# A re-planned order of a fused sparse-attention and gated-FFN kernel: free order among FFN products, the first eight in two column parts, smaller mask patterns, the fourth unit turned by crossbar transposes

## The chip, the core and the metric

One core of one Trainium2 chip runs the whole kernel in one launch. The metric is the device time of that launch in microseconds (us). The engines are PE (matrix products; its weight loads are listed as PEld), ACT, DVE and POOL for everything elementwise, and SP, which here only issues DMAs. Matrix results land in PSUM, which this kernel uses as eight buffers ("ps" 0 to 7).

## The reference, cut to what matters

There are 4 batches, 8 heads, 768 positions, head width 64. Keys come in chunks of 32. For each query and chunk an upper bound of the score is taken from the chunk's minimum and maximum; the six chunks with the highest bounds stay, and everything else, and the future, is masked.

```python
k_min, k_max = min and max of k over each chunk of 32 rows
ub = sum over d of maximum(q * k_min, q * k_max)      # bound per query and chunk
top_chunks = the 6 largest causal ub
scores = q @ k.T / 8, masked to the chosen chunks and to the past
attn = softmax(scores);  x = attn @ v                 # -> (3072, 512)
out = (sigmoid(x @ w_gate) * (x @ w_val)) @ w_out     # 512 -> 1536 -> 512
```

## The kernel before

**Units.** The 3072 rows are cut into eight units of 384 rows (three blocks of 128). Unit 0 holds the first block of batches 0 and 1 and a block 0 of batch 2, whose attention needs one key block and no selection (function first, L604). Units 1 to 7 do the selection and the attention over all earlier key blocks (attend, L847). After a unit's attention comes its FFN: for units 0 to 3 by plain products (ffn, L937, project_out, L968), for units 4 to 7 two units at a time with a Strassen-like scheme of seven products instead of eight (ffn_pair, L1016, project_pair, L1162), for which sums of weights (Sg, Sv, So) and of activations (T, S) are made on DVE or POOL.

**A unit's attention.** Keys and queries arrive as float32, are turned (units 1 and 2 by PE, kT and qT, through copies kn and qn; later batches by DVE's transposes) and copied as float16 into hk (keys) and hq (queries). Both have two halves of 64 rows: one holds the data, the other the mask. On the key side that is a fixed pattern (a large negative number where a chunk doesn't match its row), written once per batch parity, head half and pair parity: the eight hkp operations at L498, each 64 rows by 2 x 768 columns, all copied from the tile epat. On the query side it is the selection (ub, ubn, mx, ap, apt, hqm in choose, L789). A score product (sc, L863) then adds score and mask in one matmul; ACT takes the exponential (L874), POOL zeroes the future (cm, L880), PE multiplies with the values (pv, L896), DVE divides (rz, x, L913 to L915).

**Turning x for the FFN.** The FFN needs x with its 512 features on partitions. Units below XBAR = 4 are turned by PE: three transposes per head pair (xps, L929) and a copy of ACT or DVE (xT, L933). Units from 4 on are turned by a DMA transpose (L920), issued on SP.

**The FFN of units 0 to 3.** For each of 12 blocks of 128 hidden features, a product g of four matmuls of 384 columns (L952), tanh on ACT, a product v, and hg = (tanh + 1) * v on DVE (L964). All these products write a common key "ffn", so each depends on the one before: g0, v0, g1, v1, and so on, then the 9 groups o of the projection. All products read the whole xT, that is all blocks of the unit.

**Loads.** SP issues the loads of q, k and v and the stores, in one queue. The weights come as nine DMAs of POOL's queue that also convert to float16 (wg0 to wg2, wv0 to wv2, wo0 to wo2; a third of the features each); they wait until the first loads have landed (the after operations, L510).

**What sets the order.** Everything is an operation of a plan (Plan.add), with its readers, writers and the engines it may run on. The plan isn't scheduled at run time: the string ORDER (L97) names all 1982 operations in the order in which they are issued, for all engines at once, with the engine where it isn't the first one allowed (name@ENGINE) and the buffers (name:slot). Each engine executes its operations in this order and waits at each for what it needs. BEATS (L95) gives 13 groups of filler transposes of PE (beat0 to beat12, 78 in all, L473), whose results nobody reads; they keep PE running while it would wait at the start.

```python
BEATS = (20, 9, 8, 3, 3, 10, 5, 1, 2, 2, 6, 6, 3)
...
op = plan.add(f"g_{u.name}_{fb}", pe(650), product(g, wg16), reads=xt + [("wg", fb // 4)], writes=[g, "ffn"],
              prio=next_())
```

Of the kernel before, what the change touches and what calls it, by code (L numbers as in the profile page):

```python
# [15 lines left out]
XBAR = 4  # L16
# [85 lines left out]
kfT_0:5 kn_u1_1@POOL:1 qf16_0@DVE:0 qf0_1 qn_u2_3:4 kx1_u1_3 qn_u1_3:5 after3 vf_2:0 kf16_0:6 kxf0 hk1_u1_3@ACT
beat2:7 scf_0:0,4,1 v16_0_0 kT_u1_2:6 qf_u1_0 vf_1:1 kn_u2_0:0 hk0_u1_0 kx0_u1_2 hq0_u1_1@POOL expf_0_0 beat3:7
kT_u2_0:2 qT_u1_2:7 qf_u2_0:1 kf1_1 cmf_0_0 kt_u1_2:1 expf_0_1:2 q2_u2 hk1_u1_0@POOL beat4:0 pvf_0_0:3 kT_u1_1:0
qm_u1_1@ACT:0 hq1_u1_1@DVE kf0_2:0 qT_u1_3:4 after1 kx0_u1_0 vf1_2:1 qf0_2:1 kxf1:1 vc_2@ACT after6 qf1_2 qm_u1_0@ACT
kcr_f kx1_u1_2 cmf_0_1 kf1_2 qf_u1_2 kx1_u2_0:1 qf_u1_3 v11 beat5:1 pvf_0_1:7 k3_u2 qfT_1:6 kx0_u1_1 after4
qm_u1_3@ACT after5 wg0 kfT_1:4 q1_u2 rzf_0_1:0 kt_u2_0@DVE:0 qf16_1:5 k2_u2 hk0_u2_0 wv0 kt_u1_1:2 kf16_1@DVE:2 k1_u2
vf1_1:0 wg1 qm_u1_2 v_0_2:4 beat6:1 scf_1:4,6,1 qn_u2_2@DVE:3 hkp111 expf_1_1:3 v_0_3:3 beat7:1 qT_u2_2:5 qfT_2:1 hq0
vc_1@ACT kx1_u1_1 cmf_1_1 kfT_2:6 expf_1_0 rzf_0_0:1 kcr_u1@POOL xf_0_0:0 qf16_2:3 kf16_2@DVE:2 cmf_1_0 beat8:0
xpsf_0_0:3,0 xTf_0_0@ACT hkf0@DVE wv1 beat9:0 scf_2:6,1,2 qf_u2_2 xf_0_1:0 pvf_1_0:3 hk0_u1_2@ACT ub_u1:4,0 kx0_u2_0  # L110
hq0_u2_2@POOL expf_2_0 wg2 kn_u2_3@DVE:2 expf_2_1:1 hq0_u1_2@DVE pvf_1_1:6 rzf_1_0:0 hq0_u1_3 xf_1_0:1 cmf_2_1
ubn1_u1:0 qn_u2_1:0 vf1_3:3 rzf_1_1:0 hq1_u1_3 cmf_2_0 xf_1_1:2 beat10:5 qT_u2_1:0 xpsf_0_1:3 hq1 pvf_2_1:1
hq1_u2_0@POOL ubn0_u1 xpsf_1_1:6 xTf_0_1@ACT pvf_2_0:2 xpsf_1_0:7 kT_u2_3:5 hq0_u2_0 wv2 rzf_2_0:0 rzf_2_1:1
hk1_u2_0@ACT kn_u2_2@DVE:2 xf_2_0:1 wo0 qf_u2_1 v_0_1:0 xf_2_1:2 xTf_1_0@ACT beat11:4 xpsf_2_0:2 xTf_1_1@ACT ubm0_u1
xpsf_2_1:7 hk0_u1_1@ACT kn_u2_1@DVE:1 kT_u2_2:1 qT_u2_3:6 hk1_u1_1@POOL xTf_2_0 beat12:4 kT_u2_1:0 xTf_2_1 kt_u2_2:0
mx0_u1:0 wo1 hkp101@ACT g_u0_0:7,0,0 ap0_u1 wo2 apt0_u1:0 kx0_u2_2 qf_u2_3 v_u0_0:2 hq0_u1_0 hqm0_u1_2@DVE
g_u0_1:6,1,1 hq0_u2_3@POOL kx1_u2_1 hq1_u2_2@POOL v_u0_1:4 hk1_u1_2@POOL tanh_u0_1 tanh_u0_0 g_u0_2:3,2,2 hqm0_u1_0
hg_u0_1 kt_u2_1:1 v_u0_2:7 kx1_u2_2 hk0_u2_1@POOL tanh_u0_2 hg_u0_0 sc_u1_2_0:1,0 g_u0_3:3,1,3 hg_u0_2 exp_u1_2_0
k00_1:1 hq0_u2_1@DVE sc_u1_1_1:7,1 hk1_u2_1@ACT ubm1_u1 sc_u1_3_1:2,3 kx0_u2_1 cm_u1_2 sc_u1_2_1:1 sc_u1_0_2:4,2
exp_u1_3_1 v_u0_3:6 qm_u2_0@POOL:0 exp_u1_2_1 g_u0_4:2,2,4 tanh_u0_3 hq1_u1_0@POOL exp_u1_0_2 sc_u1_1_0:3 hk0_u2_2  # L120
tanh_u0_4 sc_u1_1_2:1 hkf1 sc_u1_3_0:4 exp_u1_3_0 v_u0_4:2 hk1_u2_2 kx1_u2_3 qm_u2_2@POOL exp_u1_1_0 g_u0_5:4,0,5
# [30 lines left out]
exp_u2_3_1 o1_u1_1 xf_3_1:0 k16_2_0@ACT:6 hqm0_u3_2 rz_u2_2:1 xpsf_3_1:7 kx1_2_1:1 xpsf_3_0:4 o2_u1_1 osb_u1_0 cm_u2_3
hq0_u3_2@POOL xTf_3_0@ACT xTf_3_1 sc_u3_1_0:2,1 ubn1_u3 v_2_2:4 osb_u1_1 sc_u3_0_2:4,2 x_u2_2:2 v16_1_3 exp_u3_0_2
out_u1_0 o0_u1_2:7,1 k16_2_2@DVE:4 exp_u2_2_2 v16_1_2 xps_u2_0:4 ubm1_u3 v_2_3:2 sc_u3_1_2:3 kt_2_3:0 pv_u2_3:6
xT_u2_0@ACT v16_1_0 pv_u2_2 exp_u3_1_0 q00_2 sc_u3_3_0:4,3 sc_u3_0_0:1 rz_u2_1:1 v16_1_1 x_u2_1:1 sc_u3_1_1:2
# [150 lines left out]
def kernel(  # L306
# [630 lines left out]
    def ffn(u, base, span):  # L937
# [4 lines left out]
        for fb in range(NFB):  # L942
# [6 lines left out]
            def product(t, w16, fb=fb):  # L949
                def emit(e):  # L950
                    for c in range(4):
                        nc.tensor.matmul(at(t), w16[:, c, 128 * fb:128 * fb + 128], at(u.xt)[:, c, :],  # L952
                                         start=(c == 0), stop=(c == 3))
                return emit
# [431 lines left out]
```

## Time and profile before

| what | us |
|---|---|
| times of three runs | 284.38, 285.82, 285.83 |
| median | 285.82 |
| the profiled execution | 284.64 |
| its span, first to last instruction | 282.9 |
| first FFN product (unit 0) starts | 31.05 |
| first projection of unit 0 starts | 50.8 |
| last product ends | 279.3 |

The profile is that of one execution. A stage is read from the busy times of the engines in a stretch of the span, and who waits for whom from the lists of waits. PE, DVE, ACT, POOL and SP run beside each other; an engine that is busy less than the others in a stage isn't what ends it. Matmuls overlap each other in PE's pipeline, so the distance of their starts, not their duration, is what one costs.

### The profile page before, as it was taken

The page shows a single profiled execution, that of the slowest core. Times are in us where ns is not written, and L with a number is a line of the kernel's source. Part 1 is how long each engine was busy: PE and PEld are TensorE (multiplying, and loading weights), DVE is VectorE, ACT ScalarE, POOL GpSimd, SP SyncE. Part 2 cuts the span into 40 slices and gives each one's busy share as a digit, 9 for nine tenths or more (in the row PEclk, how much of TensorE's full clock was granted, in tenths as well). Part 3 has the DMA queues.
Part 4 walks back from the last instruction along what each step waited for, and adds up shares of the span by engine and source line. Part 5 has one row for each costly group of instructions (what it writes and reads, how often), then busy time and mean ns, then how long its engine had stood idle before and what let it go on. Part 6 is the DMA issues. An engine that isn't in the chain of part 4 may idle for free.

```text
span 282.9 us, 7408 instructions
## 1 busy us (share of the span) xinstructions
PE 271.4 (96%) x2746; PEld 187.4 (66%) x2746; DVE 245.1 (87%) x665; ACT 215.5 (76%) x467; POOL 144.5 (51%) x221
## 2 busy tenths in 40 slices
PE   6998899999999999999999999999999999999994
PEld 5875565765666656754777666667666786676783
DVE  2788778529979999997998998999999999999983
ACT  4787897665667956877899998989999937778620
POOL 7468673245433765773567974415648310347020
PEclk9799999999999999999999999999999999999999
DMA  6999999999989999999920112200001013010005
GB/s 174 292 232 184 197 197 208 162 189 222 147 194 163 228 173 215 180 205 185 228 62 17 30 30 67 89 20 13 14 16 29 16 49 117 0 39 37 3 19 204
DMA packets 130035, 34.28 MB, mean 121 GB/s; under 512 B 118096, under 2 KB 127056, under 8 KB 130000
## 3 DMA queue, kind: packets, MB, share of 16 engines
q1 hardware_dynamic: 125248, 29.11, 48.9%
q0 software_dynamic: 4752, 4.72, 10.2%
q8 instruction: 21, 0.34, 0.5%
q14 instruction: 14, 0.11, 0.1%
HBM read 30.67 MB, written 6.29 MB: 131 GB/s over the span
## 4 chain that ended last, share of the span: by engine, by line
PE 77%; DVE 12%; ACT 5%; issue 3%; POOL 2%; POOLq 0%; DVEq 0%; ACTq 0%
PE g_u L952 11%; PE v_u L952 11%; PE sc_u L863 10%; PE o_u L983 8%; PE pv_u L896 6%; PE suo_u6u L1210 3%; PE suv_u6u L1069 3%; PE suo_u4u L1210 3%; PE sug_u6u L1069 2%; PE sug_u4u L1069 2%; PE suv_u4u L1069 2%; PE ube_u L801 2%; PE sro_u6u L1210 1%; PE sro_u4u L1210 1%; PE srv_u6u L1069 1%
## 5 line engine op out<-in xcount | busy, mean ns | idle before, releaser
L874 ACT ACTIVATE att_u<-sc_u 128x512 f16<-128x512 f32 (+3 forms) x184 | 90.6, 550 | 14.1 <-PE sc_u L863 13.0
L880 POOL TENSOR_SCALAR_AFFINE_SELECT att_u<-att_u 128x384 f16<-128x384 f16 (+1 forms) x56 | 29.0, 529 | 40.0 <-ACT att_u L874 34.8
L952 PE MATMUL g_u<-xT_u,wg 128*128 128x384 f16 x192 | 39.0, 326 | 1.0 <-DVE hg_u L964 0.6
L952 PE MATMUL v_u<-xT_u,wv 128*128 128x384 f16 x192 | 39.0, 326 | 0.0
L983 PE MATMUL o_u<-wo,hg_u 128*128 128x512 f16 x144 | 36.1, 379 | 0.0
L960 ACT ACTIVATE gate_u<-g_u 128x384 f16<-128x384 f32 x48 | 23.1, 494 | 12.3 <-PE g_u L952 10.6
L964 DVE SCALAR_TENSOR_TENSOR hg_u<-gate_u,v_u 128x384 f16<-128x384 f16 x48 | 25.2, 537 | 5.4 <-PE v_u L952 4.2
L896 PEld LDWEIGHTS <-att_u 128*128 128x128 f16 x640 | 25.3, 98 | 4.7 <-issue 0.2
L863 PE MATMUL sc_u<-hqo,hko 128*128 128x128 f16 (+2 forms) x220 | 27.9, 243 | 0.3 <-ACT att_u L874 0.2
L863 PE MATMUL sc_u<-hqe,hke 128*128 128x128 f16 (+2 forms) x220 | 27.4, 243 | 0.3 <-DVE ubn_u L812 0.3
L896 PE MATMUL pv_u<-v,att_u 128*128 128x65 f16 x640 | 27.6, 193 | 0.0
L952 PEld LDWEIGHTS <-wg 128*128 128x128 f16 x192 | 18.2, 98 | 11.9 <-issue 1.4
L952 PEld LDWEIGHTS <-wv 128*128 128x128 f16 x192 | 18.3, 98 | 11.1 <-DVE x_u L915 0.3
L863 PEld LDWEIGHTS <-hko 128*128 128x128 f16 x220 | 17.0, 98 | 7.3 <-issue 1.6
L863 PEld LDWEIGHTS <-hke 128*128 128x128 f16 x220 | 16.3, 98 | 7.5 <-issue 1.5
L983 PEld LDWEIGHTS <-hg_u 128*128 128x128 f16 x144 | 13.2, 98 | 10.5
L578 POOL CAST v<-v 128x512 f16<-128x512 f32 x23 | 14.8, 659 | 2.6 <-DMA v<-in_v_dram 2.1
L915 DVE TENSOR_TENSOR x_u<-pv_u,rz_u 128x384 f16<-128x384 f32 (+1 forms) x28 | 14.7, 528 | 0.6
L1192 POOL TENSOR_TENSOR v<-hgp_u 128x384 f16<-128x384 f16 x5 | 4.5, 914 | 20.3 <-PE suv_u6u L1069 13.7
L473 PE MATMUL beat<-ident 128*128 128x128 f32 x78 | 13.4, 322 | 1.4 <-POOL ident masks.py:199 1.4
L824 DVE MAX8 mx_u<-ubn_u 128x8 f32<-128x8 f32 (+16 forms) x152 | 12.7, 157 | 0.0
L473 PEld LDWEIGHTS beat<-ident 128*128 128x128 f32 x78 | 11.3, 169 | 1.7 <-POOL ident masks.py:199 1.4
(284 smaller groups left out, 695.6 us busy)
## 6 DMA issues: line engine op xcount, KB each, us to landing
v<-in_v_dram SPq DMA_DIRECT2D x23, 256.0 KB, 4.6
k<-in_k_dram SPq DMA_DIRECT2D x12, 384.0 KB, 6.4
q<-in_q_dram SPq DMA_DIRECT2D x12, 384.0 KB, 5.8
out_dram<-osb_u SPq DMA_DIRECT2D x16, 256.0 KB, 2.8
wg<-in_moe_w_gate_dram POOLq DMA_DIRECT2D x3, 512.0 KB, 13.8
wv<-in_moe_w_val_dram POOLq DMA_DIRECT2D x3, 512.0 KB, 13.8
wo<-in_moe_w_out_dram POOLq DMA_DIRECT2D x3, 512.0 KB, 20.7
out_dram<-osb_u6u SPq DMA_DIRECT2D x5, 256.0 KB, 2.0
```

The costliest lines, as they stand in the source:

```text
L473: nc.tensor.transpose(at(beat), ident32, ident32)
L578: plan.add(f"v16_{b}_{ib}", {POOL: pool(H * D)}, lambda e: nc.gpsimd.tensor_copy(v16[b % 2][:, ib, :, 0:D], at(t)), reads=[t], writes=[("v ...
L863: nc.tensor.matmul(at(t)[:, o:o + 128 * m], hk[b % 2][e_][:, p, 128 * jb:128 * jb + 128], hq[u.side][e_][:, p, 128 * x:128 * (x + m)], sta ...
L874: plan.add(f"exp_{u.name}_{h}_{y}", {ACT: act(n)}, lambda e, t=t, att=att, b0=b0, n=n: nc.scalar.activation(at(att)[:, b0:b0 + n], at(t), ...
L880: nc.gpsimd.affine_select(out=dv, in_=dv, compare_op=ALU.is_ge, fill=0.0, base=0, pattern=[[0, u.m], [1, 128]], channel_multiplier=-1)
L896: nc.tensor.matmul(at(pv)[:, last, x, :], at(att)[:, c:c + 128], v16[b % 2][:, jb, h, :], start=(jb == 0), stop=(jb == ib))
L952: nc.tensor.matmul(at(t), w16[:, c, 128 * fb:128 * fb + 128], at(u.xt)[:, c, :], start=(c == 0), stop=(c == 3))
L960: plan.add(f"tanh_{u.name}_{fb}", {ACT: act(T)}, lambda e, g=g, gate=gate: nc.scalar.activation(at(gate), at(g), AF.Tanh, scale=0.5), read ...
L964: plan.add(f"hg_{u.name}_{fb}", {DVE: dve(T)}, lambda e, w_=w_, gate=gate, hg=hg: nc.vector.scalar_tensor_tensor(at(hg), at(gate), 1.0, at ...
L983: nc.tensor.matmul(at(o), hgs[c][1][1]()[:, 128 * tb:128 * tb + 128], wo16[:, fc, lo:hi], start=(c == 0), stop=(c == NFB - 1))
L1069: nc.tensor.matmul(at(t), left[i](c), right[i](c), start=first and c == 0, stop=c == 1, skip_group_check=not first)
L1210: nc.tensor.matmul(at(t), sums[what[i][0], f][1]()[:, 128 * tb:128 * tb + 128], what[i][1](f), start=first and f == 0, stop=f == half - 1, ...
```

## The change

1. **FFN products without a chain.** g, v and the projections of units 0 to 3 no longer write "ffn"; the plan may put them in any order that their data allow.
2. **The first eight in two parts.** For unit 0, g and v of the first four feature blocks become two products each, of columns 0 to 255 (blocks of two batches) and 256 to 383 (the third), named g/gb and v/vb. Each reads only its own blocks of xT. In the new order the four v of these blocks stand first, then the four g.
3. **Patterns in pieces.** Each hkp becomes a piece of columns 0 to 511 (hkp) and one of 512 to 767 (hkq). Those of the second parity are copied from the first's and not from epat. A score product waits only for the piece that its key block lies in.
4. **XBAR = 3.** Unit 3 too is turned by DMA transposes on SP; its four groups xps and its copies are gone.
5. **POOL may do more.** The sums Sg, Sv, So and T may run on POOL. The new order uses that for T0 of units 4 and 5, T2 of units 6 and 7 and Sv2.
6. **A new ORDER** of 1995 operations and new BEATS: 14 groups, 69 fillers, four of them (beat13) after the first v products. About 160 operations are on another engine than before. wv0 is issued before wg0. On SP, v_0_4 and v_0_5 come after the first store, three v loads of batch 2 after its q loads, and unit 3's transposes between batch 3's k and q loads.

```diff
-XBAR = 4
+XBAR = 3
...
-BEATS = (20, 9, 8, 3, 3, 10, 5, 1, 2, 2, 6, 6, 3)
+BEATS = (17, 4, 10, 2, 4, 5, 2, 7, 4, 2, 1, 3, 4, 4)
...
-                const(f"hkp{i}{e_}{o}", {DVE: dve(2 * S, 4, 64), POOL: pool(2 * S), ACT: act(2 * S, False, 64)},
-                      lambda e, i=i, e_=e_, o=o: copy(e, hk[i][e_][MASK[e_], o::2], at(epat)[:, o].rearrange(
-                          "p c s -> p (c s)").unsqueeze(1).to_broadcast([64, NP // 2, S])),
-                      reads=[epat], writes=[("hkp", i, e_, p) for p in range(o, NP, 2)], prio=0.3 + 0.2 * i, port=True)
+                for w, cols in enumerate((slice(0, 512), slice(512, S))):
+                    n = 2 * (cols.stop - cols.start)
+                    const(f"hk{'pq'[w]}{i}{e_}{o}", {DVE: dve(n, 4, 64), POOL: pool(n), ACT: act(n, False, 64)},
+                          lambda e, i=i, e_=e_, o=o, cols=cols: copy(e, hk[i][e_][MASK[e_], o::2, cols],
+                              hk[0][e_][MASK[e_], o::2, cols] if i else at(epat)[:, o].rearrange(
+                              "p c s -> p (c s)")[:, cols].unsqueeze(1).to_broadcast([64, NP // 2, cols.stop - cols.start])),
+                          reads=[("hkp", 0, e_, p, w) for p in range(o, NP, 2)] if i else [epat],
+                          writes=[("hkp", i, e_, p, w) for p in range(o, NP, 2)], prio=0.3 + 0.2 * i + 0.3 * w, port=True)
...
-                reads += [("hkp", b % 2, e_, p) for b, _, _, _ in u.banks[y]] + [("hq", u.side, e_, p), ("hqm", u.side, e_, p)]
+                reads += [("hkp", b % 2, e_, p, int(jb > 3)) for b, jb, _, _ in u.banks[y]] + [("hq", u.side, e_, p), ("hqm", u.side, e_, p)]
...
-            op = plan.add(f"g_{u.name}_{fb}", pe(650), product(g, wg16), reads=xt + [("wg", fb // 4)], writes=[g, "ffn"],
-                          prio=next_())
-            plan.hold(op, gate)
-            plan.hold(op, hg)
+            early = u.i == 0 and fb < 4
+            parts = [("", 0, 256, xt[:0] + [(u.xt, c, x) for c in range(4) for x in range(2)]),
+                     ("b", 256, T, [(u.xt, c, 2) for c in range(4)])] if early else [("", 0, T, xt)]
+
+            for tag, lo, hi, need in parts:
+                op = plan.add(f"g{tag}_{u.name}_{fb}", pe(4 * ((hi - lo) / 2.4 + 2.5)), product(g, wg16, lo=lo, hi=hi),
+                              reads=need + [("wg", fb // 4)] + ([g] if lo else []), writes=[g], prio=next_())
+                if not lo:
+                    plan.hold(op, gate)
+                    plan.hold(op, hg)
...
-            op = plan.add(f"S{name}{i}", {DVE: dve(n, 1.8)}, lambda e, i=i, x=x, op=op, y=y: nc.vector.tensor_tensor(at(t)[:, i], x(), y(), op),
+            op = plan.add(f"S{name}{i}", {DVE: dve(n, 1.8), POOL: (3640, 3660)}, lambda e, i=i, x=x, op=op, y=y: (
+                nc.vector if e == DVE else nc.gpsimd).tensor_tensor(at(t)[:, i], x(), y(), op),
```

The order around the first FFN products, after, cut to PE's operations there (with the weights' DMAs):

```
... qT_u2_0 ... wg0 ... qfT_2 ... scf_2 ... ub_u1 ... xpsf_1_1 ... wv1 ... beat12 xpsf_2_1 kT_u2_1 v_u0_0
xpsf_2_0 v_u0_1 v_u0_2 wg2 vb_u0_0 vb_u0_2 wv2 v_u0_3 vb_u0_1 vb_u0_3 beat13 g_u0_3 gb_u0_3 g_u0_2 gb_u0_2
g_u0_0 gb_u0_0 sc_u1_0_0 g_u0_1 gb_u0_1 wo0 sc_u1_0_2 kT_u2_0 sc_u1_2_0 kT_u2_3 g_u0_4 ...
```

And around unit 3's transposes (SP, PE):

```
... k11_3 ... v_2_0 ... k10_3 ... k00_3 ... k01_3 ... xT_u3_1 ... out_u1_2 ... xT_u3_2 ... xT_u3_0 ... xT_u3_3 ...
sc_u4_2_0 sc_u4_2_2 o2_u2_1 sc_u4_3_2 q01_3 o1_u2_0 o2_u2_0 sc_u4_1_3 out_u2_0 o0_u2_2 o1_u2_2 q10_3 sc_u4_6_2
sc_u4_1_1 sc_u4_1_0 sc_u4_3_0 sc_u4_6_3 sc_u4_6_1 o2_u2_2 pv_u4_2 sc_u4_3_3 sc_u4_0_0 g_u3_1 ...
```

More of the change, by code (lines that the diff above doesn't have):

```diff
@@ L102 @@
[L102 to L121, printed above, removed]
@@ L152 @@
[L152 to L155, printed above, removed]
-exp_u3_3_0 sc_u3_2_0:0,0 kx1_2_2 xps_u2_2:5 o1_u1_2 xT_u2_2@ACT exp_u3_1_1 kx0_2_3 xps_u2_1:5 exp_u3_1_2 o2_u1_2
@@ L282 @@
-Q3_u6u7_1 out_u7_1 G3_u6u7_0 Q4_u6u7_0 G1_u6u7_1 out_u6_1 F2_u6u7_0 out_u7_0
+v10 q1_u1:0 epat0:0 ident kf1_0:0 ap0 vf1_2:0 epat k2_u1 kcr0 kf0_0 q0_u1 k1_u1 hkp011@ACT hkq010 qf0_0:1 hkp010@POOL
+qf1_0 qn_u1_1:1 q3_u1 hkp001 hkp000@POOL vf_0:2 beat0:7 kfT_0:0 kn_u1_2@DVE:2 qT_u1_1:1 q2_u1 qn_u1_0@POOL:3
+kn_u1_1@DVE:4 kf16_0:5 k3_u1 kT_u1_2:2 kT_u1_1:3 kf0_1:0 qf_u1_1:0 kt_u1_1:0 kx1_u1_1:0 k0_u1 qfT_0:1 kxf1:1 qf1_1:3
+hk1_u1_1@POOL qf16_0:4 ident16 vf_1:0 ap1 qn_u1_3:2 beat1:7 scf_0:1,4,1 qT_u1_0:5 expf_0_0 v16_0_0 qT_u1_3:6
@@ new lines @@
+rzf_2_1:0 kn_u2_2:3 kn_u2_0@POOL:1 rzf_1_1:1 v_0_3:2 xf_1_1:0 hk1_u1_3@ACT beat11:6 kT_u2_2:4 qn_u2_1@POOL:6 pvf_2_0:1
+hq0_u1_0 hkf0 qT_u2_1:5 rzf_2_0:1 xpsf_1_1:0 xf_2_0:1 wv1 xTf_1_1@ACT xf_2_1:0 qm_u2_3@ACT:0 xTf_0_1 qm_u2_0@ACT
+beat12:6 xpsf_2_1:2 hk0_u1_1@POOL ubn0_u1 kT_u2_1:0 xTf_2_1@ACT v_u0_0:7 hkp101@POOL ubm0_u1 kt_u2_1:1 mx0_u1:0
+xpsf_2_0:2 hk0_u2_1@ACT v_u0_1:3 qf_u2_1 xTf_2_0 v_u0_2:1 wg2 kx1_u2_1:1 kt_u2_2:0 vb_u0_0 hq1_u2_3@DVE hk1_u2_2@ACT
+vb_u0_2 ubm1_u1 wv2 v_u0_3:5 ap0_u1 apt0_u1:0 vb_u0_1 vb_u0_3 kx1_u2_2 hqm0_u1_0@ACT hqm0_u1_2@DVE kx0_u2_2
@@ new lines @@
+hkp111@POOL beat13:6 g_u0_3:2,0,0 qm_u2_2@ACT kx0_u2_1 gb_u0_3 g_u0_2:4,1,1 tanh_u0_3 hq1_u1_0@POOL gb_u0_2 k01_1:0
+g_u0_0:0,2,2 hg_u0_3 hkq000@POOL tanh_u0_2 gb_u0_0 sc_u1_0_0:5,3 kn_u2_3:2 qm_u2_1@POOL hg_u0_2 g_u0_1:4,0,3 tanh_u0_0
+gb_u0_1 exp_u1_0_0 wo0 hg_u0_0 sc_u1_0_2:1 kT_u2_0:2 sc_u1_2_0:0,0 exp_u1_0_2 kT_u2_3:6 tanh_u0_1 hq0_u2_1@POOL
+g_u0_4:5,1,4 exp_u1_2_0 wo1 kt_u2_3@DVE:2 hg_u0_1 g_u0_7:4,2,5 tanh_u0_4 wo2 kx1_u2_3 sc_u1_3_2:3,1 g_u0_6:0,0,6
+kx0_u2_0 exp_u1_3_2 vf1_3:2 kx0_u2_3 hkq110@POOL sc_u1_2_1:3 kx1_u2_0 sc_u1_3_1:6 tanh_u0_6 g_u0_5:5,3,7 hk0_u2_2
```

353 lines of the change are left out of this document (185 added, 168 removed).

## The prediction

> **What bounds the kernel now.** I read the page's engine totals first, then the busy time of each engine by stage.
>
> ```profile
> PE 271.4 (96%) x2746; PEld 187.4 (66%) x2746; DVE 245.1 (87%) x665; ACT 215.5 (76%) x467; POOL 144.5 (51%) x221
> ```
> ```profile
> 0.00:31.05 31.05, 25.54 (x234) 21.21 (x235) 22.13 (x68) 22.76 (x47) 22.11 (x46) 0.95 1.02 218
> 31.05:50.98 19.93, 19.59 (x155) 11.53 (x153) 15.74 (x65) 16.41 (x35) 10.24 (x19) 1.00 1.27 201
> 50.98:143.00 92.02, 91.06 (x954) 58.44 (x953) 78.47 (x223) 66.33 (x140) 48.98 (x76) 1.00 1.01 192
> 183.00:266.00 83.00, 82.17 (x748) 57.13 (x747) 80.19 (x173) 69.44 (x164) 33.92 (x41) 1.00 0.11 33
> ```
> ```profile
> 31.05:279.30 248.25, 245.85 (x2514) 166.15 (x2511) 222.98 (x600) 192.34 (x420) 122.35 (x175) 1.00 0.55 109
> ```
>
> The columns are the stretch, its length, the busy time of PE, PEld, DVE, ACT and POOL, PE's clock, the DMA share and GB/s. From 31.05 on, where the first FFN product starts, PE is busy 245.85 of 248.25 us: all visible idle there is 2.4 us. So after the head a change is worth what it takes off PE, plus at most those 2.4 us. The first 31.05 us are different, as PE's own list of groups and its timeline at the end of the head show:
>
> ```profile
> L473 PE MATMUL beat<-ident 128*128 128x128 f32 x78 | 13.4, 322 | 1.4 <-POOL ident masks.py:199 1.4
> ```
> ```profile
> 29.61 0.61 PE L680 MATMUL xpsf<-ident,xf 128*128 128x128 f16 x4 [0.49 <-DVE xf L673]
> 30.07 0.39 PE L700 MATMUL kT_u<-ident,kn_u 128*128 128x128 f32 x2
> 30.29 0.38 PE L700 MATMUL qT_u<-ident,qn_u 128*128 128x128 f32 x2
> 30.51 0.49 PE L473 MATMUL beat<-ident 128*128 128x128 f32 x3
> 30.84 0.38 PE L700 MATMUL kT_u<-ident,kn_u 128*128 128x128 f32 x2
> 31.05 0.81 PE L952 MATMUL g_u<-xT_u,wg 128*128 128x384 f16 x4
> 31.70 0.81 PE L952 MATMUL v_u<-xT_u,wv 128*128 128x384 f16 x4
> ```
>
> All 78 fillers ("beats", whose result nobody reads) lie in the head: 13.4 us of its 25.54 busy ones, beside 5.5 us of idle time. Real PE work is about 12 of 31 us. The other engines set the head's length: DVE 22.13, ACT 22.76 and POOL 22.11 of 31.05 us, with loads at a DMA share of 1.02. The end, 279.30 to 282.9, is a last copy and stores, which the change leaves alone.
>
> **The change part by part.** Sums are made against the profiled execution, 284.64 us (span 282.9 and 1.74 around it). The median of the three times shown, 285.82, is 1.18 higher; I give forecasts on the scale of that median.
>
> *Patterns.* Before, eight copies of 1536 columns fill the pattern rows. They cost by these rows (two of DVE's three are of the first kind, the third took 0.670):
>
> ```profile
> L359 DVE COPY hko<-epat x2: 544/548/552, 3.1 to 20.9; 64x1536 f16<-64x1536 f16 x2
> L357 ACT COPY hke<-epat x2: 1470/1470/1470, 4.5 to 30.9; 64x1536 f16<-64x1536 f16 x2
> L363 POOL COPY hke<-epat x1: 1462/1462/1462, 7.1 to 7.1; 64x1536 f16<-64x1536 f16 x1
> ```
>
> Three on ACT, two on POOL and three on DVE make 4.41 + 2.92 + 1.77 = 9.1 us; one of ACT's runs at 30.9, so 7.6 lie ahead of the first product. After, each is a piece of two thirds and one of a third, and the order puts only seven pieces ahead of that product: ACT and POOL pieces at about 0.98 and 0.49 by proportion, DVE's at 0.4 and 0.2, which makes 4.5 us. That takes 3.1 us off three engines. The written order also moves other work of unit 2 (copies, reductions, query copies of about 0.4 each) behind the first product: some fourteen go, seven come, about 2.5 us net. Together 5.6 us less; spread over three engines the head is **1.8 us** shorter. The bounds: 0 if loads set the head, and at most 4.1, because the first weights were issued at 18.05 and the quickest landing took 8.9 (26.95):
>
> ```profile
> 18.05 1.00 POOL L517 DMA_DIRECT2D wg<-in_moe_w_gate_dram  x1
> ...
> DMA to landing us min/median/max: 8.9/13.8/16.1
> ```
>
> I take 1.8, which is what the engines' rows give, since ACT and DVE are the busier side there.
>
> *Products in two parts, wv first.* Eight products become 256 + 128 columns: 32 more matmuls. Four of 384 columns start 0.65 apart from the next four (31.05, 31.70), four of 512 in the projections 0.86; the slope leaves about 3 ns per matmul that isn't columns, so **+0.1 us**. The first part needs only two of the three x blocks; but PE runs in the written order, where v_u0_0 stands behind xpsf_2_1, so the split brings little by itself. That v needs wv alone, and wv is now issued first, is what matches the weights' landings; g starts four products (2.6 us) later, when the second megabyte is there.
>
> *What moves behind the first product* is now in the stage where PE has no idle time: two key turns (kT_u2_0, kT_u2_3; 0.21 each, 30.84 to 31.05), half of an xpsf pair group (0.1) and four fillers (0.11 each, 30.51 to 30.84): **+1.0 us**.
>
> *Fourth unit by crossbar.* Four groups of three PE turns go, with two copies on ACT and two on DVE, which the rest of that stage hides anyway.
>
> ```profile
> 131.65 0.33 PE L929 MATMUL xps_u<-ident,x_u 128*128 128x128 f16 x3
> 131.81 1.03 PE L983 MATMUL o_u<-wo,hg_u 128*128 128x512 f16 x4
> ```
>
> 0.16 us each: **-0.65 us**. Instead SP issues four DMA transposes, in the row below 1.2 us of issue each. Queued behind them on SP stand the q loads of batch 3 and stores; the first reader of these loads, a turn for unit 6, stands nine FFN products and the work counted below later in the order, over 14 us of PE time.
>
> ```profile
> L920 SPq DMA_TRANSPOSE xT_u<-x_u x8: 1179/1237/2074, 148.0 to 176.2; - x8
> DMA to landing us min/median/max: 2.3/2.4/3.9
> ```
>
> Between the last one, xT_u3_3, and its first reader, g_u3_1, PE's order holds six projections (0.86), twelve score groups (0.22) and one value group (0.4): 8.2 us of cover for a landing of 2.4, if the DMA engines are free.
>
> *No fixed order, and other engines for single steps.* Counting by engine over the whole order with the rows' durations, DVE loses about 5 us, ACT gains 2.6 and POOL 8. From 183 to 266 DVE is busy 80.19 of 83.00, so that is the right direction; PE there waits only 0.83. Steps of 768 and 1536 columns that go to POOL (T0, T2, Sv2) aren't shown on POOL; its nearest row is
>
> ```profile
> L1192 POOL TENSOR_TENSOR v<-v,hg_u 128x384 f16<-128x384 f16 x6 | 6.1, 1021 | 0.7 <-PE suv_u4u L1069 0.6
> ```
>
> so 2 and 4 us by proportion, each with more PE work than that between it and its reader. Of the 2.4 us of idle after the head I let the freer order recover a third: **-0.8** (bounds: -2.4 if all goes; +6.8 if the whole runs at the idle rate of its worst long stretch, below).
>
> Sum: -1.8 + 0.1 + 1.0 - 0.65 - 0.8 = **-2.15 us**: 282.5 for the profiled execution, **283.7** on the median's scale. The fillers themselves are costed at nothing beyond the four that move: in the head they only fill waits.
>
> *A rule that speaks against it.* The granted clock fell once:
>
> ```profile
> 4.79:8.20 3.41, 1.69 (x12) 1.03 (x10) 0.51 (x1) 2.19 (x3) 2.96 (x4) 1.00 1.02 296
> 8.20:11.62 3.42, 3.32 (x16) 3.32 (x17) 3.35 (x10) 2.38 (x4) 0.51 (x2) 0.50 1.14 304
> ```
>
> A stretch of 3.41 us with PE half busy was followed by one at 0.50; all later ones ran at 1.00. With fewer fillers a second such stretch can occur in the head. At half clock 3.4 us of PE work lose 1.7. The Trainium skill, "TensorE: Matmul & The Clock Gate", section "Part 1: The HAM clock gate (the "warmup" mystery)", has this as a rule: after an idle window of about 3.4 us the array runs at half its clock, and the windows run freely. By that rule the trace agrees with the fall at 8.20, though PE was half busy rather than idle.
>
> **The rivals.**
>
> *The head's gain is given back to the loads.* From 31 to 143 us the DMA share is 1.27 and 1.01, so the inputs of units 3 to 5 can't come earlier by themselves. POOL already waits for keys:
>
> ```profile
> POOL k L363 <- DMA k<-in_k_dram: 2.6, 2, 1.5
> ```
>
> Also v_0_5 and v_0_4 now stand behind the first store on SP. Then PE waits later for what it won: 283.7 + 1.8 = 285.5, no change. Against it: the q loads of batch 2 now stand ahead of three v loads that were in front of them.
>
> *The clock falls twice in the head:* +1.7 where the fillers' place is real work, 285.4, no change.
>
> *Crossbar transposes land late (the other side).* They are issued right behind the four key loads of batch 3, in a stage whose DMA engines are full:
>
> ```profile
> 118.00:135.00 17.00, 16.82 (x165) 9.64 (x161) 15.25 (x58) 13.18 (x25) 9.44 (x13) 1.00 1.01 194
> ...
> k<-in_k_dram SPq DMA_DIRECT2D x12, 384.0 KB, 6.4
> ...
> DMA to landing us min/median/max: 4.6/6.4/23.5
> ```
>
> 384 KB at 194 GB/s take 2 us, so four in front make a landing of 8 + 2.4 = 10.4, and the worst key load took 23.5. From 8.2 us on g_u3_1 waits, and with it everything behind on PE; the result is slower than no change when the landing takes over 11.8. At 15, the middle of 6.4 and 23.5, the stall is 6.8: 290.5. Against it: the last transposes are issued some us after those loads, and the queue drains between.
>
> *The new order makes PE wait more.* PE takes its work in the written order, so each mis-costed step on DVE or POOL is a stall. The worst long stretch of before:
>
> ```profile
> 100.00:117.00 17.00, 16.37 (x164) 10.44 (x169) 15.60 (x40) 12.21 (x26) 12.08 (x19) 1.00 1.03 194
> ```
>
> That is 3.7% idle; over 248 us it would be 9.2 instead of 2.4, +6.8. At half of that excess it is 283.7 + 0.8 + 3.4 = 287.9. It decides from an idle time of about 6 us after the head.
>
> **How the numbers follow.** Forecast 283.7: 0.50 (its own range 280.5 to 284.4). Loads take the gain back, 285.5: 0.18. Clock, 285.4: 0.04. Late transposes, 290.5: 0.10. More waits in the order, 287.9: 0.18. A measurement of this kernel tells about 0.5% (1.4 us) from no change; faster by more 0.50, within 0.22, slower 0.28. The low end, 280.5, is a head shorter by the full 4.1 us with a little of the idle time (0.04 below). The high end, 288.5, takes in the order's waits and leaves out most of the late transposes and the worst of the waits (0.15).
>
> **What would show it.** Right: the first v_u0 product at 29 to 29.5 us (31.05 before, 0.2 either way), no xps_u in unit 3's stage, transposes landing in under 8 us with no PE wait before g_u3_1, PE idle after the first product at most 2.4 us, DVE busy near 240 in all. Wrong: a wait of PE for DMA or for POOL casts between 60 and 75; a PE gap of over 1 us ahead of unit 3's FFN with SP's transposes as releaser; PEclk under 0.9 in slices after the second; or visible PE idle of over 5 us between 50 and 183.

## The result, and the profile after

The changed kernel takes 288.19 us (median of 10 runs, 285.65 to 289.37), the kernel before 285.85: a ratio of 1.0063 [1.0034, 1.0092], slower by 0.6%. The forecast was 283.7. Some executions are in a slower state, and the ratio is taken over the others alone, so it isn't the quotient of the two medians, which is 1.0082. The profiled execution took 288.49 us, its span 286.8.

The views of the kernel after that answer to those of before: engine totals, the stretches (columns as in the prediction), PE's first FFN product and the largest PE waits. In the pair stages, Sv2 and Sv3 are two of the four sums of the value weights, T0 to T3 the four sums of activations; the products that read them (sug, srg, suv and so on) are called pair products here.

```profile
PE 270.2 (94%) x2757; PEld 186.8 (65%) x2757; DVE 246.3 (86%) x660; ACT 218.5 (76%) x473; POOL 151.7 (53%) x224
```
```profile
0.00:28.10 28.10, 22.45 (x215) 17.70 (x216) 18.59 (x52) 21.36 (x44) 18.22 (x42) 1.00 0.98 216
183.00:266.00 83.00, 80.21 (x725) 55.52 (x724) 78.00 (x164) 67.40 (x158) 35.09 (x42) 0.98 0.11 35
28.10:283.40 255.30, 247.80 (x2544) 169.07 (x2541) 227.69 (x609) 196.79 (x429) 133.51 (x183) 0.99 0.55 109
```
```profile
28.10 0.60 PE L958 MATMUL v_u<-xT_u,wv 128*128 128x256 f16 x4
```
```profile
PE sug_u4u L1084 <- DVE x_u L921: 2.7, 1, 2.7
PE sug_u6u L1084 <- DVE osb_u L1238: 1.8, 1, 1.8
...
PE srg_u6u L1084 <- DVE T_u6u L1049: 0.9, 1, 0.9
```

The head is 2.95 us shorter (28.10 for 31.05). But from the first product to PE's end, PE now has 7.5 us of visible idle (255.30 less 247.80), where it had 2.4. Three waits of the pair stages make 5.4 of it. DVE was to come near 240 us; it shows 246.3 with five instructions fewer, so its operations got longer. The timelines of DVE, POOL and PE ahead of the longest wait show which:

```profile
174.15 1.28 DVE L1025 TENSOR_TENSOR Sg<-Sg,wg 128x1536 f16<-128x1536 f16 x1
174.58 3.80 POOL L1025 TENSOR_TENSOR Sv<-wv 128x1536 f16<-128x1536 f16 x1
175.35 3.85 DVE L1025 TENSOR_TENSOR Sv<-wv,Sv 128x1536 f16<-128x1536 f16 x1
...
179.12 1.46 DVE L1049 TENSOR_TENSOR T_u4u<-xT_u,T_u4u 128x768 f16<-128x768 f16 x2
...
181.33 0.50 PE L1084 MATMUL sug_u4u<-xT_u,wg 128*128 128x384 f16 x2 [2.72 <-DVE x_u L921]
```

Sv3 on DVE takes 3.85 beside Sv2 on POOL. In the kernel before, with nothing on POOL beside it, it took 0.91:

```profile
173.58 0.91 DVE L1011 TENSOR_TENSOR Sv<-wv,Sv 128x1536 f16<-128x1536 f16 x1
```

In the changed kernel it ends 0.82 us after POOL's sum (179.20 and 178.38), which is nearly its own length. T1 and T3 stand behind it on DVE, and x_u behind them (180.72 to 181.28). The division x_u is the last reader of the PSUM buffer that the order gives the waiting product, so it is rightly named as the releaser. Then PE pays a second time, as the granted clock in the stretches after the wait shows:

```profile
178.00:181.40 3.40, 0.68 (x5) 0.23 (x4) 3.33 (x6) 0.91 (x2) 1.57 (x2) 1.00 0.00 0
...
182.50:185.80 3.30, 3.30 (x16) 1.90 (x15) 2.25 (x6) 2.59 (x7) 0.00 (x0) 0.50 0.28 83
```

3.3 us at half clock lose 1.65, by estimate. Of the ten runs, four show a mean clock of 0.994 and average 288.9; six show 1.00 and average 287.2.

**Theory A**: the sums put on POOL and DVE's sums of two SBUF operands get in each other's way; what stands behind them on DVE comes late, PE waits, and the clock falls. **Rivals**: (B) the new written order makes DVE late by itself; (C) only the half clock costs; (D) the transposes of the last pair set that wait; (E) the fourth unit's transposes or the loads behind them cost.

### The profile page after: what moved, and what is told of

The parts are those of the page before. It is cut to its first block, busy times and chain, and to the rows that moved or that the text cites. A ratio compares the mean times of both kernels' runs of the same rounds, so it can differ in the third digit from the quotient of the medians.

```text
span 286.8 us, 7427 instructions
## 1 busy us (share of the span) xinstructions
PE 270.2 (94%) x2757; PEld 186.8 (65%) x2757; DVE 246.3 (86%) x660; ACT 218.5 (76%) x473; POOL 151.7 (53%) x224
## 4 chain that ended last, share of the span: by engine, by line
PE 68%; DVE 20%; DMA 5%; issue 2%; ACT 2%; SPq 1%; POOL 0%; DVEq 0%; ACTq 0%; POOLq 0%
PE sc_u L869 10%; PE g_u L958 10%; PE v_u L958 9%; PE o_u L996 9%; PE pv_u L902 5%; PE ube_u L807 3%; PE sug_u6u L1084 2%; DVE hg_u L1114 2%; DMA q<-in_q_dram 2%; PE suv_u6u L1084 2%; PE sug_u4u L1084 2%; PE suo_u6u L1226 2%; DVE hgp_u L1114 2%; DMA kq_u<-in_k_dram 1%; DMA xT_u6u<-x_u 1%
## 5 line engine op out<-in xcount | busy, mean ns | idle before, releaser
L958 PE MATMUL g_u<-xT_u,wg 128*128 128x384 f16 (+2 forms) x208 | 36.8, 314 | 0.4 <-DVE kcr L592 0.4
L958 PE MATMUL v_u<-xT_u,wv 128*128 128x384 f16 (+2 forms) x208 | 36.7, 314 | 0.0
L996 PE MATMUL o_u<-wo,hg_u 128*128 128x512 f16 x144 | 35.2, 379 | 0.0
L958 PEld LDWEIGHTS <-wg 128*128 128x128 f16 x208 | 19.1, 98 | 10.4 <-issue 0.7
L958 PEld LDWEIGHTS <-wv 128*128 128x128 f16 x208 | 19.0, 98 | 9.2
L869 PEld LDWEIGHTS <-hke 128*128 128x128 f16 x220 | 16.9, 98 | 8.1 <-DVE x_u L921 0.8
L1084 PEld LDWEIGHTS <-Sg 128*128 128x128 f16 x96 | 9.4, 102 | 6.5 <-DVE T_u6u L1049 1.1
L475 PE MATMUL beat<-ident 128*128 128x128 f32 x69 | 11.7, 309 | 1.8 <-POOL ident masks.py:199 1.6
L774 DVE STREAM_TRANSPOSE qf_u<-q 128x384 f32<-128x384 f32 (+2 forms) x28 | 11.7, 437 | 1.5 <-DMA q<-in_q_dram 1.1
```

Of the source, the lines that this page charges most:

```text
L869: nc.tensor.matmul(at(t)[:, o:o + 128 * m], hk[b % 2][e_][:, p, 128 * jb:128 * jb + 128], hq[u.side][e_][:, p, 128 * x:128 * (x + m)], sta ...
L958: nc.tensor.matmul(at(t)[:, lo:hi], w16[:, c, 128 * fb:128 * fb + 128], at(u.xt)[:, c, lo:hi], start=(c == 0), stop=(c == 3))
L996: nc.tensor.matmul(at(o), hgs[c][1][1]()[:, 128 * tb:128 * tb + 128], wo16[:, fc, lo:hi], start=(c == 0), stop=(c == NFB - 1))
L1084: nc.tensor.matmul(at(t), left[i](c), right[i](c), start=first and c == 0, stop=c == 1, skip_group_check=not first)
```

## The experiments

Ratios are to the kernel before on the same chip (its medians: 285.31 for the first three below and for the kernel before with Sv2 on POOL; 284.63 for the three smaller sums, the early Sv2, the crossbar and the mask pieces; 284.96 for the last three and the second profile of the early Sv2).

### Sv2 back on DVE

```diff
-... P6g_u4u5_0 osb_u3_1 Sv2@POOL P2g_u4u5_1
+... P6g_u4u5_0 osb_u3_1 Sv2 P2g_u4u5_1
```

> The changed kernel with one sum of the pair stage, Sv2 (1536 columns), on DVE instead of POOL, at the same place of the written order. Theory A (POOL's sum and DVE's Sv3 beside it stretch each other, 3.80 and 3.85 us; that makes T1 and T3 late, PE waits 2.7 us for x_u and then runs about 1.3 us at half clock): Sv3 takes under 1.5 us again, the wait of sug_u4u5 falls below 0.7 us, and the time falls by 2.5 to 4, to 284.2 to 285.7 by the medians (288.19 for the changed kernel, 285.85 for the kernel before). Rival B (the new order itself makes DVE late there, whatever POOL does): DVE gets 1 to 1.5 us more in the same stretch, the wait stays at 2 us or more, and the time stays within 0.7 of 288.2.

Measured: 284.74, ratio 0.9977 [0.9955, 0.9998]. DVE's Sv3, and two lines of PE's and ACT's timeline in the head:

```profile
176.67 0.95 DVE L1025 TENSOR_TENSOR Sv<-wv,Sv 128x1536 f16<-128x1536 f16 x1
...
36.04 0.41 ACT L359 COPY kn_u<-kq_u 128x256 f32<-128x256 f32 x1 [2.23 <-DMA kq_u<-in_k_dram]
...
36.88 0.38 PE L869 MATMUL sc_u<-hqe,hke 128*128 128x128 f16 x4 [1.74 <-ACT gate_u L972]
```

Sv3 is short again, up to 200 us no pair product waits for more than 0.16, and the sign of the change turns: A, against B. The head shows what a still earlier first product (27.86) meets: ACT waits 2.23 us for a load of keys, the gate stands behind it, and PE waits 1.74.

### T2 of the last pair back on DVE

```diff
-... G3_u4u5_1 T2_u6u7@POOL P2v_u6u7_0
+... G3_u4u5_1 T2_u6u7 P2v_u6u7_0
```

> The changed kernel with only T2 of the last pair on DVE instead of POOL. Theory A (POOL's T2, 1.95 us, stretched DVE's T3 beside it to 1.87, and PE waited 1.8 us for it): that wait falls under 0.8 us and the time falls by 1 to 1.8, to 286.4 to 287.2. Rival D (the end of that chain is set by the crossbar transpose of x_u7, which landed at 233.7, just ahead of T1): the wait and the time stay as they are, 288.2 within 0.5, since DVE has one more sum to do behind the landing.

Measured: 286.28, ratio 1.0049 [1.0026, 1.0072]; the interval overlaps that of the changed kernel, so the times alone don't settle it. The trace does: T1 and T3 take 1.15 together (2.46 before the edit, beside T2 on POOL), and the wait of 1.8, whose releaser osb_u runs on DVE right behind T3, is down to 0.2. D falls: the landing still holds T1 up, by 0.37, and PE doesn't notice. The changed kernel's lines, then this one's:

```profile
233.70 2.46 DVE L1049 TENSOR_TENSOR T_u6u<-xT_u6u,T_u6u 128x768 f16<-128x768 f16 x2 [0.66 <-DMA xT_u6u<-x_u]
233.79 1.95 POOL L1049 TENSOR_TENSOR T_u6u<-xT_u6u 128x768 f16<-128x768 f16 x1 [10.02 <-issue]
```
```profile
232.89 1.15 DVE L1049 TENSOR_TENSOR T_u6u<-xT_u6u,T_u6u 128x768 f16<-128x768 f16 x2 [0.37 <-DMA xT_u6u<-x_u]
```

The wait of 2.7 is still in this kernel, and nine of its twelve runs have a mean clock of 0.994 or less. With Sv2 on DVE two of twelve had.

### All three sums back on DVE

```diff
-... T0_u4u5@POOL:0 ... Sv2@POOL ... T2_u6u7@POOL ...
+... T0_u4u5:0 ... Sv2 ... T2_u6u7 ...
```

> The changed kernel with all three sums that the change put on POOL ahead of the pair stages (T0 of the first pair, Sv2, T2 of the last pair) back on DVE. Theory A: the gains of the two single steps add, 3.5 to 5.5 us: 282.7 to 284.7, faster than the kernel before, with the first FFN product still near 28 us. Rival B: DVE, busy 86%, takes the three sums (3 us in all) on the chain instead, and the time stays at 287 or more. Rival C (only the half clock after the long wait costs): as sv2_dve alone, no further gain from T2.

Measured: 282.48, ratio 0.9900 [0.9871, 0.9928]: 1% faster than the kernel before. Against the changed kernel that is 0.9900/1.0063, 1.6% or 4.6 us, from three words of the order. B falls, since everything else of the new order is still there, and C, since T0 and T2 bring more than Sv2 alone (0.9977). What is left of the waits has the same form, T0 of the last pair beside one of POOL's smaller sums, as before the edit:

```profile
218.78 0.50 PE L1084 MATMUL srg_u6u<-T_u6u,Sg 128*128 128x384 f16 x2 [0.85 <-DVE T_u6u L1049]
```

### Three smaller sums on DVE as well

```diff
-... S2_u4u5_3@POOL ... S4_u4u5_1@POOL ... S3_u4u5_3@POOL ...
+... S2_u4u5_3 ... S4_u4u5_1 ... S3_u4u5_3 ...
```

> The changed kernel with the three sums on DVE (282.48) and, in addition, three of POOL's smaller sums (S2 and S3 of part 3, S4 of part 1, 384 columns) on DVE. In the run with the three sums PE waited 0.85 us for T0 of the last pair, which took 1.26 us instead of 0.55 beside POOL's sum (1.22), and a product on DVE beside it took 1.29 instead of 0.55. Theory A: three sums of 0.35 more on DVE, 1.5 us given back by the two stretched ones, the wait goes: 281.5 to 282. Rival (DVE is the bound there, 19.7 busy of 20 us from 210 to 230, and has no room for them): 282.5 to 283.5.

Measured: 281.72, ratio 0.9887 [0.9855, 0.9919], the fastest kernel of this study. T0 takes its own time and its wait is gone:

```profile
215.37 0.54 DVE L1049 TENSOR_TENSOR T_u6u<-xT_u6u 128x768 f16<-128x768 f16 x1
```

The step from 0.9900 lies inside the intervals; in the trace another wait (0.63, ahead of srv_u6u) takes part of its place. The engine totals show what DVE's list is worth: against the changed kernel DVE has six sums more and is busy 4.2 us less (242.1 for 246.3).

```profile
PE 270.3 (96%) x2757; PEld 188.3 (67%) x2757; DVE 242.1 (86%) x666; ACT 218.2 (78%) x473; POOL 143.6 (51%) x218
```

### The kernel before, with Sv2 on POOL

```diff
-... P2v_u4u5_0 Sv2 E1v_u4u5_0:5 ...
+... P2v_u4u5_0 Sv2@POOL E1v_u4u5_0:5 ...
```

Here and in the next experiment the code of the sums also takes over from the change that they may run on POOL.

> The kernel before with nothing changed but Sv2, which goes to POOL at its place in the order. Theory A (a two-input sum on POOL is by itself enough to hold up DVE's sums): Sv2 takes 3 to 4 us on POOL, DVE instructions with two inputs beside it take two to four times as long, and the kernel is slower by 0.5 to 4, depending on what lies beside it: 286.3 to 289.8. Rival (POOL's sum costs DVE nothing; the order of the changed kernel is what hurts): DVE loses 1 us of work and the time is 285.85 or less.

Measured: 284.87, ratio 0.9984 [0.9959, 1.0010]: no difference. My first form of theory A, that such a sum on POOL does harm by itself, fell here. The timeline sharpened it:

```profile
184.27 3.09 POOL L1011 TENSOR_TENSOR Sv<-wv 128x1536 f16<-128x1536 f16 x1
```
```profile
185.57 0.55 DVE L1084 TENSOR_TENSOR c1g_u4u<-c1g_u4u,srg_u4u 128x384 f32<-128x384 f32 x1
186.04 1.64 DVE L829 TENSOR_TENSOR ap<-ubn_u,mx_u 128x288 f16<-128x288 f32 x1
187.60 0.54 DVE L1084 TENSOR_TENSOR c0v_u4u<-c0v_u4u,sqv_u4u 128x384 f32<-128x384 f32 x1
```

DVE's adds of a PSUM tile (0.54 to 0.55) run beside POOL's sum untouched. The one operation with two SBUF operands, ap, takes 1.64 instead of 0.45 and ends 0.32 after POOL's sum (187.68 and 187.36). Nothing on PE waited for that ap.

### The same, with Sv2 where DVE has its sums

```diff
-... hk1_3_2 mx1_u7:0 ... P2v_u4u5_0 Sv2 E1v_u4u5_0:5 ...
+... hk1_3_2 Sv2@POOL mx1_u7:0 ... P2v_u4u5_0 E1v_u4u5_0:5 ...
```

> The kernel before with Sv2 on POOL, but early in POOL's queue, where POOL idled 3.56 us (from 171.9): there DVE's Sv3 runs beside it (0.91 us by itself), with T1 and T3 and the first pair product behind. With Sv2 late on POOL (3.09 us from 184.27, beside DVE adds that read PSUM and took 0.55 as ever) the kernel before stayed at 284.87 against 285.31. Theory A, sharpened (a sum of two SBUF operands on DVE and one on POOL at the same time hold each other up; other DVE work is not touched): Sv3 takes over 2 us, T1 to T3 come 1.5 to 2.5 us later, PE waits 1 to 2.5 us ahead of the pair's T products, 286.3 to 287.8. Rival (POOL's sum does no harm in the order of the kernel before): 285.3 within 0.7.

Measured: 287.06, ratio 1.0082 [1.0051, 1.0113], so 2.4 us slower. One of its nine executions, the profiled one, took 713 us for a reason that stays open, so the kernel was profiled once more:

> The kernel before with Sv2 early on POOL once more, for its trace alone (eight of its nine times lay between 286.10 and 288.92; the profiled one was 713 us with PE busy 99% and shows nothing of the collision). Theory A: Sv2 on POOL at about 171.9 and Sv3 on DVE beside it take about as long as each other, over 2 us, and a PE wait of 1 to 2.5 us stands ahead of the first pair's T products. Rival: Sv3 stays at 0.9 us, and the 2.4 us come from another place, such as a mask select on POOL that now waits behind Sv2 and holds up the scores.

Measured: 287.03. The timelines of POOL, DVE and PE:

```profile
171.61 3.67 POOL L1011 TENSOR_TENSOR Sv<-wv 128x1536 f16<-128x1536 f16 x1
...
173.22 2.88 DVE L1011 TENSOR_TENSOR Sv<-wv,Sv 128x1536 f16<-128x1536 f16 x1
...
177.80 1.02 PE L983 MATMUL o_u<-wo,hg_u 128*128 128x512 f16 x4 [1.00 <-DVE x_u L915]
179.21 0.48 PE L1069 MATMUL srg_u4u<-T_u4u,Sg 128*128 128x384 f16 x2 [0.39 <-DVE T_u4u L1034]
...
185.21 0.50 PE L1069 MATMUL srg_u4u<-xT_u,Sg 128*128 128x384 f16 x2 [0.39 <-DVE Sg L1011]
```

Sv3 takes 2.88 and ends 0.82 after POOL's sum (176.10 and 175.28). Three new waits, 1.78 us together, stand behind it on PE. The same sum on the same engine is free in one place and costs 2.4 us in the other; what differs is DVE's work beside it.

### The fourth unit's crossbar transposes alone

```diff
-XBAR = 4
+XBAR = 3
-xps_u3_1:4,0 ... xT_u3_1@ACT ... xps_u3_0:2 ... xps_u3_3:1 ... xT_u3_3 ... xps_u3_2:7 ... xT_u3_2@ACT xT_u3_0
+... xT_u3_1:0 ... xT_u3_3 ... xT_u3_2 xT_u3_0
```

> The kernel before with the fourth unit's x turned by crossbar transposes and nothing else changed: 12 PE turns of 0.16 go. The prediction's step: -0.65, 284.6 to 284.8, no PE wait ahead of that unit's products. Rival E (the transposes stand behind full DMA queues on SP, or hold up the loads behind them): a PE wait of 1 us or more ahead of unit 3's products or in the stages after it, 286 or more. Third: the 12 turns lay beside idle time of PE, and nothing moves (285.3).

Measured: 293.89, ratio 1.0310 [1.0270, 1.0351]: 9 us slower. The list of waits, and SP's timeline:

```profile
PE g_u L952 <- DMA xT_u<-x_u: 5.8, 1, 5.8
```
```profile
130.72 2.38 SPq L562 DMA_DIRECT2D q<-in_q_dram  x2
133.15 6.62 SPq L920 DMA_TRANSPOSE xT_u<-x_u  x3
```

E is right for the kernel before: three transposes, issued behind two loads, take 6.62 us of SP, and g_u3 follows close behind. A wait of 1.3 and PE's clock of 0.71 from 140 to 150 come on top. In the changed kernel the same transposes cost nothing to be seen, since its order issues them from 119.07 on, well ahead of g_u3:

```profile
L926 SPq DMA_TRANSPOSE xT_u<-x_u x12: 1177/1202/2518, 119.1 to 172.7; - x12
...
DMA to landing us min/median/max: 2.3/2.4/4.3
```

### The mask pieces alone

```diff
-... v_u0_0:2 hq0_u1_0 ... v_u0_3:6 qm_u2_0@POOL:0 ...
+... v_u0_0:2 hkq010 hkq001@ACT hkq011@POOL hkq000 hq0_u1_0 ...
+... v_u0_3:6 hkq100@POOL hkq110@ACT hkq111 hkq101@ACT qm_u2_0@POOL:0 ...
```

and the code of the pieces from the change.

> The kernel before with the mask patterns in pieces and nothing else: the two-thirds pieces at the old places and engines, the eight pieces of one third behind the first FFN products. The prediction's step took 3.1 us off three engines ahead of the first product for the change's order, a third of which for the head; here one third of the 7.6 us goes (2.5 us over three engines), so by the same working the first product comes 0.8 us earlier and the time falls by 0.8, to 284.5. If another chain sets the head (the loads, or the chain of the first keys), the first product stays at 30.6 to 31.1 and the time at 285.3 within 0.5.

Measured: 287.58, ratio 1.0101 [1.0062, 1.0140]. The first product doesn't move, and behind it PE waits for operations that the pieces hold up on ACT and DVE (timelines of PE and ACT):

```profile
30.72 0.81 PE L956 MATMUL g_u<-xT_u,wg 128*128 128x384 f16 x4
...
35.72 0.38 PE L867 MATMUL sc_u<-hqe,hke 128*128 128x128 f16 x4 [0.94 <-DVE kx_u L590]
39.95 0.72 PE L867 MATMUL sc_u<-hqe,hke 128*128 128x128 f16 x9 [1.23 <-ACT gate_u L964]
```
```profile
37.76 0.62 ACT L357 COPY hko<-hko 64x512 f16<-64x512 f16 x1
38.39 0.61 ACT L357 COPY hke<-hke 64x512 f16<-64x512 f16 x1
39.03 0.49 ACT L878 ACTIVATE att_u<-sc_u 128x384 f16<-128x384 f32 x1
39.42 0.48 ACT L964 ACTIVATE gate_u<-g_u 128x384 f16<-128x384 f32 x1
```

So engine time taken out of the head isn't the head's length, and a piece moved to the wrong place costs more than it took. My choice of place was rough; the change spreads its pieces over lines 98 to 139 of its kernel.

The last three experiments edit the fastest kernel, the changed one with the six sums on DVE.

### The pieces put back ahead

```diff
-... v_u0_0:7 hkp101@POOL ... hkp111@POOL ... hkq000@POOL ... hkq110@POOL ... hkq100@ACT ... hkp110@POOL ... hkp100 ... hkq101@POOL ... hkq111@ACT
+... hkq001@ACT hkq000@POOL hkp101@POOL ... wg1 hkp111@POOL hkp100 ... hkf0 hkp110@POOL hkq100@ACT ...
+... qm_u2_0@ACT hkq110@POOL hkq101@POOL hkq111@ACT ...
```

> The changed kernel with the six sums on DVE (281.72 against 284.63), and with the nine mask pieces that its order leaves until after the first FFN product put ahead of it again: 4.4 us more on POOL, 1.0 on ACT, 0.4 on DVE. The prediction's step (engine time of the head, spread over three engines, sets the head): the first product comes 1.9 us later (28.9 to about 30.8) and the time rises by 1.9, to 283.6. Rival (pieces moved alone gained nothing in the kernel before, where the first product stayed at 30.72: the patterns are not what sets the head, POOL has room): first product within 0.7, time 281.7 within 0.7.

Measured: 283.70, ratio 0.9951 [0.9939, 0.9963], 0.64% or 1.8 us above the kernel with the six sums. The time is that of the prediction's step; the way isn't: the first product is 0.63 later instead of 1.9, and most of the rest is a wait of 1.0 behind it that the kernel with the six sums doesn't have.

```profile
29.57 0.60 PE L958 MATMUL v_u<-xT_u,wv 128*128 128x256 f16 x4
```
```profile
PE ube_u L807 <- DVE kcr L599: 1.0, 1, 1.0
```

### The first products whole

```diff
-            early = u.i == 0 and fb < 4
+            early = False
-... v_u0_0:7 ... v_u0_1:3 ... v_u0_2:1 ... vb_u0_0 ... vb_u0_2 ... v_u0_3:5 ... vb_u0_1 vb_u0_3 ... g_u0_3:2,0,0 ... gb_u0_3 ...
+... v_u0_0:7 ... v_u0_2:1 ... v_u0_1:3 v_u0_3:5 ... g_u0_3:2,0,0 ...
```

> The changed kernel with the six sums on DVE, but with its eight first products whole (384 columns), each at the place of its second part: behind the third x block. The prediction's step: the split costs 0.1 and PE stands behind xpsf_2_1 anyway, so 281.6 within 0.5. Rival (starting four v products on two of three x blocks fills time in which PE would wait for the third block): first product 0.5 to 1 us later, PE waits, 282.3 to 283.3.

Measured: 281.85, ratio 0.9908 [0.9876, 0.9940], beside 0.9887 [0.9855, 0.9919]: no difference that can be told. PE waits 0.76 for the third block, and has the 32 matmuls less.

```profile
29.29 2.76 PE L958 MATMUL v_u<-xT_u,wv 128*128 128x384 f16 x16 [0.76 <-DVE xT_u L361]
```

### Fewer fillers

```diff
-BEATS = (17, 4, 10, 2, 4, 5, 2, 7, 4, 2, 1, 3, 4, 4)
+BEATS = (1,) * 14
```

> The changed kernel with the six sums on DVE and 14 fillers instead of 69 (one in each group; nothing reads them). The prediction costed the fillers at nothing: time 281.7 within 0.5, and the first product at the same 28.9 within 0.7, since other engines set the head. Rival (the clock, as in the stretch behind 8.2 us in the profile of the kernel before): one or two half-clock stretches appear in the head, and the time rises by 1 to 3.5.

Measured: 283.72, ratio 0.9950 [0.9931, 0.9969], 1.8 us above the kernel with its 69 fillers, and all twelve runs show a mean clock of 0.994 or less. Two stretches of the head (columns as above):

```profile
13.60:17.00 3.40, 1.31 (x12) 0.95 (x13) 2.52 (x9) 3.33 (x9) 1.11 (x5) 0.90 1.03 242
17.00:20.40 3.40, 3.19 (x19) 2.60 (x17) 2.20 (x5) 2.45 (x7) 1.53 (x4) 0.60 0.85 212
```

The fillers hold the clock, as the rival said. That the half clock makes up all of the 1.8 isn't shown: the first product stands at 29.52, only 0.58 later, and a PE wait of 0.68 at 135.10, which the kernel with 69 fillers doesn't have, is another part. The Trainium skill, "TensorE: Matmul & The Clock Gate", section "Part 1: The HAM clock gate (the "warmup" mystery)", has an idle window of about 3.4 us halve the clock; here PE was not idle in the stretches right ahead of a fall, but busy 1.36 us (12.90 to 16.31 of this run) and 1.11 us (179.03 to 182.44 of the changed kernel). Stretches with 1.65 and 1.68 us (from 233.64 in the changed kernel, from 14.50 in the one with the six sums) were followed by full clock.

## Why the prediction was wrong, point by point

**Head, -1.8.** Right in size; the reason is not borne out. In the five profiles with the changed head as it is, the first product stands at 27.71, 27.86, 28.10, 28.94 and 30.30; the kernel before and its variants have 30.53 to 31.05. The pieces alone brought nothing in the old order, and put back in the new one they moved the first product by 0.63. What else in the order of the head makes it shorter was not taken apart, and why the first product varies between 27.71 and 30.30 with the same head stays open.

**Split, +0.1.** Costed as next to nothing, and no difference could be told (281.85 whole, 281.72 split). From the two distances shown, 0.65 and 0.86, the part of a matmul that isn't columns comes out at about 5 ns and not 3, 0.16 us in all, which changes nothing.

**Work moved behind the first product, +1.0; crossbar, -0.65; and what is idle.** Together with the split and the -0.8 the sum after the head was -0.35. With the six sums on DVE it is 251.76 (280.7 less 28.94) for 251.85 (282.9 less 31.05): -0.1. The whole span is 2.2 shorter there; the sum was -2.15. That the two meet so closely is luck, given how the first product varies. The crossbar's share was not measured by itself in the new order; in the old one it costs 9 us, since the cover of 8.2 us that I counted is the new order's.

**No fixed order, and other engines, -0.8: the step that failed.** PE's idle time after the head was to fall from 2.4 to 1.6 us; it rose to 7.5. The step gave T0, T2 and Sv2 on POOL 2 and 4 us and asked only whether their readers came later. They do. The durations were right too (Sv2 3.80, T2 1.95). What I left out is what DVE does meanwhile: an operation of DVE with two SBUF operands that meets POOL's sum stands still until that is done. From the traces: 2.7 us of waiting by Sv2, 1.8 by T2, about 0.5 by T0 (from the 401st value matmul, pv_u, to the first pair product it is 9.99 us with T0 on POOL, 167.80 to 177.79, and 9.52 without, 169.58 to 179.10), and 1.65 for the half clock in those runs that have it. That is 5.0 to 6.7; taking the three sums back brought 4.6 by the ratios, so what these waits cost doesn't add up in full. "DVE loses about 5 us, that is the right direction" was wrong for the same reason: the work left DVE's list and not its time. The profile of the kernel before could have told it. There Sg takes 1.57 us on DVE beside a copy on POOL, for 0.96 otherwise, and ends 0.80 after the copies:

```profile
180.64 2.10 POOL L363 COPY hqe<-apt_u 64x768 f16<-64x768 f16 x2 [3.64 <-DVE apt_u L835]
...
181.97 1.57 DVE L1011 TENSOR_TENSOR Sg<-wg,Sg 128x1536 f16<-128x1536 f16 x1
```

**Fillers at nothing.** For the nine that the change drops this wasn't tested by itself. As a rule it is wrong: 55 of them are worth 1.8 us.

**The rivals.** "The new order makes PE wait more" (287.9) came true, with its mechanism, a mis-costed step on DVE or POOL that becomes a stall; that the step was the three sums it didn't say. "The head's gain is given back to the loads" is seen in part, as ACT's wait for keys whenever the first product came by 27.86. "Crossbar transposes late" didn't happen here, and did with the old order.

## What to carry to other kernels

Before a sum goes from DVE to POOL, look at what DVE runs in those microseconds: in these traces a DVE operation with two SBUF operands waited POOL's whole instruction out, and one that read PSUM didn't. Place POOL's long sums beside PSUM work, or leave them. And a change of many parts can be a good one with a bad word in it: undo the parts one by one before it is given up.

## What the runs showed of the hardware

A DVE operation with two SBUF operands and an instruction of POOL beside it did not share in these traces: the one that came second waited. If they shared, DVE's would be partly done when POOL's ends; instead it still needs nearly its whole length. Five cases, each with DVE's own length and the time by which it ended after POOL's instruction: Sv3 0.91 and 0.82 (changed kernel), Sv3 0.91 and 0.82 (Sv2 early), ap 0.45 and 0.32, T0 0.54 and 0.42, a product hg 0.54 and 0.41. POOL waits in the same way: Sv2, 3.09 us beside PSUM work, took 3.80 when it started at 174.58 with Sg on DVE until 175.43. The last two of the five are these, from the changed kernel:

```profile
219.07 0.91 POOL L1208 TENSOR_TENSOR v<-hg_u,v 128x384 f16<-128x384 f16 x1
219.10 1.29 DVE L1114 SCALAR_TENSOR_TENSOR hg_u<-gate_u4u,c0v_u4u 128x384 f16<-128x384 f16 x1
219.94 1.22 POOL L1208 TENSOR_TENSOR hgp_u<-hg_u,hgp_u 128x384 f16<-128x384 f16 x1
220.32 1.26 DVE L1049 TENSOR_TENSOR T_u6u<-xT_u6u 128x768 f16<-128x768 f16 x1
```

The Trainium skill says this in "SBUF — State Buffer", section "🔬 SBUF: two separate sides": DVE with two SBUF inputs and GpSimd take one pair of ports as an exclusive lock, and the loser waits for the whole instruction. The runs agree with it, and it was the rule to weigh here.
